# Forty products of the identity in TensorE's pauses of the first attention, and one early power on GpSimd

## The chip, the core and the metric

The kernel runs on one core of a Trainium2 chip. The core has five engines that run their own instruction streams and meet at semaphores: TensorE (PE in the profile; its weight loads are shown as PEld), VectorE (DVE), ScalarE (ACT), GpSimd (POOL) and SyncE (SP, which here only issues DMAs). The metric is the device time of one execution in microseconds; less is better. Times are given for the median of several executions, and the profile is of a single one.

## The reference

The first half is an attention between 512 tokens and 32 state rows for each of 8 batches and 8 heads of width 64, in both directions. Its output is rearranged to 4352 rows of 512 and goes through a gated feed-forward layer of width 1536.

```
scores = scale * x @ state^T            # B,H,512,32
xread  = softmax(scores) @ state
sread  = softmax(scale * state @ x^T) @ x
rows   = concat(xread, sread), heads joined        # (8*544, 512)
xn     = rows / sqrt(mean(rows^2) + 1e-6) * rms_g
out    = (silu(xn @ w_gate) * (xn @ w_val)) @ w_out
```

The weights come as 64-bit floating-point numbers and are turned into 32-bit ones on the chip.

## The kernel before

Batch 0 stands apart from the others, since the weights are still being fetched and converted while it runs. Its work is cut into streams, Python generators that issue a few instructions and yield. The string `ORDER` (lines 22 to 28) is the schedule, written out by hand: one letter is one step of one stream. TensorE, VectorE and ScalarE execute their instructions in exactly this order; each engine takes its own instructions one after the other, so one that waits holds up all behind it. GpSimd's and SyncE's instructions are placed by the framework.

The streams that matter here:

- `a`, `tokens_read(0)`: transposes the state rows (line 268) and the tokens (278), scores (287), a softmax over the 32 state rows (VectorE: 298 transposition, 307 maximum, 309, 318 sum, 320 to 323, 325 transposition back; ScalarE: 300 copy, 311 exponential), the read (332), and the mean square of the read: ScalarE squares (339), VectorE adds (342), TensorE sums over partitions (346), VectorE adds the epsilon (350), GpSimd raises to the power -1/2 (250), TensorE spreads the result along rows (257), and VectorE multiplies the weights of attention by it (356).
- `s`, `states_read(0)`: the softmax in the other direction (368 maximum, 374 exponential), its transposition (381) with the copy out (383), the read (393), its scaling (400), and a transposition (404, copied by 406).
- `e` and `d`, `exponents` and `values`: the conversion of 18 weight pieces, three steps on ScalarE (195, 197, 200) and four on VectorE (221, 224, 228, 233) for each piece. The raw pieces are loaded four ahead (166). ScalarE's and VectorE's halves of a piece meet in two buffers named `ex` and two named `top`; the first weights go to `w_m`, the output weights to `wo`, and converted `w_m` is also written to DRAM as `w_d` (237).
- `v`: the state rows times the converted weights (450), copied to `v` by ScalarE (461).
- `h`, `t`, `u`: gate and value products of one of the 12 blocks of the hidden layer from `aT_s` and `v` (492), silu (498), product of both (502).
- `p`: the projection to the output (690), accumulated in four PSUM banks taken from the pools `fx`, `fz`, `fx` and `fy` (687).
- `A` and `S`: the two attention streams of batch 1.

Batches 1 to 7 run in a second hand-written order, `PERIOD`, with a matrix product of seven block products instead of eight (lines 596 and 750), and the state rows of all batches follow at the end. PSUM banks named `at` and `pv` come two to a pool, so a product into a third one waits until the first has been copied out. The tile `ident` is the 128x128 identity for transpositions, built by GpSimd at the start; `mhalf` holds -1/2 and `ones` holds 1.

Of the kernel before, what the change touches and what calls it, by code (L numbers as in the profile page):

```python
# [8 lines left out]
F32 = mybir.dt.float32  # L9
# [3 lines left out]
ALU = mybir.AluOpType  # L13
# [4 lines left out]
P = 128  # L18
# [1 line left out]
W_BUFS = 3  # L20

ORDER = (
    "aaaaaaaaddaaaaaaeaseeaasadsassssdsaaaasaeadesaeeasdasaaeadeadaaaddeeasedaadsadae"
    "edvvavdadeaAhdeeddtdAdAAhueheAeedtddphAedvdvduvdphedeAedtdhApeehddeuAdddeAhdedvd"
    "tudvvpeAAAAdhdAAteAehuhpddephepdeAdAeApAdteedAAvvveAdpudAAephtdSdhAdphdeAueedhAd"
    "eAteudddeeSppAddAAdppAdAdevApvdveehhAdthAudhpdeddeedeAdteAupvdvdvphedAAtdShhutSA"
    "hpukSSSkkkwSwkpSkpwpSSckSScckkpcSwkkkwwww"
)

PERIOD = (  # L30
# [12 lines left out]
def kernel(  # L43
# [20 lines left out]
    VE, SE, GE, TE = nc.vector, nc.scalar, nc.gpsimd, nc.tensor  # L64
# [5 lines left out]
    NC = S // P  # L70
# [7 lines left out]
    consts = ctx.enter_context(tc.tile_pool(name="consts", bufs=1))  # L78
# [9 lines left out]
    fz = ctx.enter_context(tc.tile_pool(name="fz", bufs=1, space=PSUM))  # L88
# [11 lines left out]
    def load_state(b):  # L100

        rows[b] = two.tile([P, 2, D], F32, name="rows")
        for j in range(4):
            src = state[b, 2 * j:2 * j + 2].rearrange("e n d -> n e d")
            nc.sync.dma_start(out=rows[b][Ns * j:Ns * j + Ns], in_=src)
# [8 lines left out]
    ident = consts.tile([P, P], F32, name="ident")  # L114
    make_identity(nc, ident)
    mhalf = consts.tile([P, NC], F32, name="mhalf")
    GE.memset(mhalf, -0.5)
    ones = consts.tile([P, 1], F32, name="ones")
    GE.memset(ones, 1.0)
    bounds = consts.tile([P, 2], F32, name="bounds")  # L120
    GE.memset(bounds[:, 0:1], 1151.0 + 7.5 / 16)
    GE.memset(bounds[:, 1:2], 255.0 * (1 << 23))
# [58 lines left out]
    def exponents():  # L181

        for k in range(len(pieces)):
            for a in parts(k):
                if k not in raw:
                    yield from range(3)
                    continue
                if a.start == 0:  # L190
                    exs[k] = conv.tile([P, 8 * P], I32, name="ex")
                ex = exs[k][:, columns(k, a)]
                hi = raw[k][:, columns(k, a), 1]
                half = ex.bitcast(U16).rearrange("p (f two) -> p f two", two=2)[:, :, 1]
                SE.activation(out=ex.bitcast(F32), in_=hi.bitcast(F32), func=ACTF.Abs)
                yield
                SE.activation(out=ex, in_=half, func=ACTF.Relu, scale=-1.0 / 16,
                              bias=bounds[:, 0:1])
                yield
                SE.activation(out=ex, in_=ex, func=ACTF.Relu, scale=-float(1 << 23),  # L200
                              bias=bounds[:, 1:2])
                yield
# [235 lines left out]
    def own_weights(b, mp):  # L438


        pv = []

        def products():
            w = w_sb.pop(b * (NM // 2) + mp)
            for e in range(2):
                pv.append(vps.tile([P, 4 * P], F32, name="pv") if b and mp % 2 == 0 else
                          aps.tile([P, 4 * P], F32, name="at"))
            for j in range(4):
                for e in range(2):
                    TE.matmul(out=pv[e][Ns * j:Ns * j + Ns, :],  # L450
                              lhsT=stT_g[b][D * e:D * e + D, j, :],
                              rhs=w[D * e:D * e + D, j].rearrange("p m k f -> p (m k f)"),
                              start=True, stop=True)
            fetch(b * (NM // 2) + mp + W_BUFS)
            yield

        def copies():
            v = (seven["v"] if b else v_0).tile([P, 2, 2, 2, P], F32, name="v")
            v_sb[b, mp] = v, None
            for e in range(2):  # L460
                SE.copy(v[:, e].rearrange("p m k f -> p (m k f)"), pv[e])  # L461
                yield
            if b:
                more_of_v(b, mp)
                yield

        return products(), copies()
# [215 lines left out]
    def project_as_ready(banks):  # L683


        for f in (fx, fz, fx, fy):
            banks.append(f.tile([P, DM], F32, name="f"))

        def part(m, r):
            TE.matmul(out=banks[r], lhsT=hb[:, m, P * r:P * r + P], rhs=wo[:, m, :],  # L690
                      start=(m == 0), stop=(m == NM - 1))

        for m in range(NM - 2):
            for r in range(4):
                part(m, r)
                if r % 2:
                    yield
        for r in range(4):
            part(NM - 2, r)
            part(NM - 1, r)  # L700
            yield

    def projected(banks, store):
        spare = seven["s"].rearrange("p (r k) f -> p r (k f)", r=3)
        for r in range(4):
            ot = spare[:, r] if r < 3 else two.tile([P, DM], F32, name="ot", tag="g")
            SE.copy(ot, banks[r])
            store(r, 0, DM, ot)
            yield
# [11 lines left out]
    def weight_sums():  # L721

        t1, t2, t4 = (seven["t"][:, i] for i in range(3))
        for k in range(0, HM, 2):
            def blk(i, j):
                return wo[:, HM * i + k:HM * i + k + 2, HD * j:HD * j + HD]
            for dst, a, b in ((t1[:, k:k + 2], blk(0, 1), blk(0, 0)),
                              (t2[:, k:k + 2], blk(1, 1), t1[:, k:k + 2]),
                              (blk(0, 1), blk(1, 1), blk(0, 1)),
                              (t4[:, k:k + 2], blk(1, 0), t2[:, k:k + 2])):  # L730
                VE.tensor_tensor(out=dst, in0=a, in1=b, op=ALU.subtract)
                yield
# [81 lines left out]
    def store_tokens(b):  # L814
        def store(r, c0, n, ot):
            r0 = T * b + P * r
            nc.sync.dma_start(out=out[r0:r0 + P, c0:c0 + n], in_=ot)
        return store
# [7 lines left out]
    done = object()  # L826

    def of_batch_0(part):

        for m in range(NM):  # L830
            if m not in parts_0:
                parts_0[m] = hidden(m, lambda e, k, m=m: v_sb[0, m // 2][0][:, e, m % 2, k, :],
                                    [aT_s[0][:, e, :] for e in range(2)])
            yield from parts_0[m][part]

    def first_of_batch(b):
        for mp in range(2):
            for part in own_weights(b, mp):
                yield from part

    def first_products(b, own):
        slot_sums(b)
        yield
        for part in own:
            yield from part[0]
# [15 lines left out]
    for k in range(1, RAW_AHEAD):  # L861
# [3 lines left out]
    streams = {"a": tokens_read(0), "s": states_read(0), "A": tokens_read(1), "S": states_read(1),  # L865
               "e": exponents(), "d": values(),
               "v": (step for mp in range(NM // 2) for part in own_weights(0, mp) for step in part),
               "h": of_batch_0(0), "t": of_batch_0(1), "u": of_batch_0(2),
               "p": project_as_ready(banks_0), "c": projected(banks_0, store_tokens(0)),
               "w": first_of_batch(1), "k": weight_sums()}  # L870
    by_hand = dict(engines={mybir.EngineType.PE, mybir.EngineType.DVE,
                            mybir.EngineType.Activation})
    with tc.manual_schedule(**by_hand):
        for stream in ORDER:
# [2 lines left out]
                open_late()  # L877
                slot_sums(1)
            next(streams[stream])
    assert all(next(stream, done) is done for stream in streams.values())  # L880
    load_state(2)
    load_x(2)

    for b in range(1, B):
        if b + 2 < B:
# [3 lines left out]
        p, c, k = project_seven(S, store_tokens(b))  # L889
# [3 lines left out]
        streams = {"h": h, "t": t, "u": u, "p": p, "c": c, "k": k,  # L893
                   "v": (step for part in own for step in part[0]),
                   "x": (step for part in own + then for step in part[1])}
        if b + 1 < B:
            streams.update(a=tokens_read(b + 1), s=states_read(b + 1),
                           w=first_products(b + 1, then))
# [12 lines left out]
    p, c, k = project_seven(NT, store_states, nc.scalar)  # L911
    streams = {"h": h, "t": t, "u": u, "p": p, "c": c, "k": k, "y": sums_of_w(range(1, NM // 2))}
# [33 lines left out]
```

## Time and profile before

| | |
|---|---|
| median of six runs | 802.4 us |
| lowest, highest | 802.0, 803.26 us |
| profiled execution, device time | 803.26 us |
| its span, first to last instruction | 801.5 us |
| mean granted TensorE clock | 0.987 |
| TensorE busy | 776.5 us (97%) |
| VectorE busy | 515.0 us (64%) |
| ScalarE busy | 347.1 us (43%) |
| GpSimd busy | 178.0 us (22%) |

A slice of the page's picture is one fortieth of the span, 20 us. A digit is the busy share of an engine in tenths; the row PEclk is the granted TensorE clock in tenths of full speed. The profile counts the passes of a product: one 32-bit product makes two passes, so eight products of line 450 are written "x16". A row of the timeline gives start and length in us, engine, line, what is written from what, and in square brackets the engine's idle time ahead of it and what ended it. Ends of matrix products are modelled, so rows that follow one another overlap a little.

### The profile page before, as it was taken

The page shows a single profiled execution, that of the slowest core. Times are in us where ns is not written, and L with a number is a line of the kernel's source. Part 1 is how long each engine was busy: PE and PEld are TensorE (multiplying, and loading weights), DVE is VectorE, ACT ScalarE, POOL GpSimd, SP SyncE. Part 2 cuts the span into 40 slices and gives each one's busy share as a digit, 9 for nine tenths or more (in the row PEclk, how much of TensorE's full clock was granted, in tenths as well). Part 3 has the DMA queues.
Part 4 walks back from the last instruction along what each step waited for, and adds up shares of the span by engine and source line. Part 5 has one row for each costly group of instructions (what it writes and reads, how often), then busy time and mean ns, then how long its engine had stood idle before and what let it go on. Part 6 is the DMA issues. An engine that isn't in the chain of part 4 may idle for free.

```text
span 801.5 us, 12112 instructions
## 1 busy us (share of the span) xinstructions
PE 776.5 (97%) x4822; PEld 594.2 (74%) x4822; DVE 515.0 (64%) x786; ACT 347.1 (43%) x572; POOL 178.0 (22%) x215
## 2 busy tenths in 40 slices
PE   4599999999999999999999999999999999999998
PEld 2244444788878887888778887888788877888996
DVE  4989996588337851787358833785178735891461
ACT  5888874563145322542246314532254224510320
POOL 0000003530145004510443014500451044400000
PEclk9589999999999999999999999999999999999999
DMA  9788744710182006500361008200540025101311
GB/s 294 232 272 311 265 160 163 247 67 0 33 287 105 1 16 205 204 1 14 100 237 75 1 30 287 108 1 14 172 184 2 13 104 179 74 0 47 112 54 27
DMA packets 61592, 94.11 MB, mean 117 GB/s; under 512 B 38752, under 2 KB 46432, under 8 KB 54624
## 3 DMA queue, kind: packets, MB, share of 16 engines
q1 hardware_dynamic: 59360, 92.75, 33.7%
q8 instruction: 38, 0.62, 0.3%
q10 hardware_dynamic: 2176, 0.59, 0.3%
q14 instruction: 18, 0.15, 0.1%
HBM read 78.12 MB, written 15.20 MB: 116 GB/s over the span
## 4 chain that ended last, share of the span: by engine, by line
PE 94%; DVE 4%; issue 0%; ACT 0%; DMA 0%; SPq 0%; DVEq 0%
PE f L596 37%; PE f L750 35%; PE f L690 5%; PE pv L492 4%; PE at L450 3%; PE pv L450 3%; PE at L278 2%; PE at L287 1%; PE at L332 1%; PE at L346 1%; PE at L393 1%; DVE ex L228 1%; PE at L381 1%; DVE raw L224 1%; PE at L257 1%
## 5 line engine op out<-in xcount | busy, mean ns | idle before, releaser
L750 PE MATMUL f<-wo,hb 128*128 128x256 f32 x540 | 124.2, 382 | 0.4 <-ACT ot L787 0.2
L658 DVE TENSOR_TENSOR g<-g,f 128x512 f32<-128x512 f32 (+1 forms) x96 | 62.7, 654 | 90.1 <-PE f L596 86.6
L596 PE MATMUL f<-aT_s,v 128*128 128x256 f32 x504 | 119.5, 380 | 0.0
L750 PEld LDWEIGHTS f<-wo,hb 128*128 128x128 f32 x540 | 101.4, 190 | 20.1 <-ACT ot L787 6.9
L596 PEld LDWEIGHTS f<-aT_s,v 128*128 128x128 f32 x504 | 93.8, 190 | 17.4 <-issue 5.2
L250 POOL TENSOR_TENSOR ri<-ss,mhalf 128x4 f32<-128x4 f32 x8 | 9.1, 1142 | 365.5 <-DVE ss L350 365.5
L596 PE MATMUL f<-aT_t,vs 128*128 128x256 f32 x336 | 87.2, 382 | 0.0
L750 PE MATMUL f<-wt,hs 128*128 128x256 f32 x360 | 80.4, 379 | 0.0
L649 ACT ACTIVATE hb<-g 128x1024 f32<-128x1024 f32 (+1 forms) x48 | 48.2, 1004 | 63.0 <-DVE g L658 63.0
L750 PEld LDWEIGHTS f<-wt,hs 128*128 128x128 f32 x360 | 68.3, 190 | 9.5 <-issue 0.2
L787 ACT COPY ot<-f 128x256 f32<-128x256 f32 x60 | 21.5, 372 | 122.6 <-PE f L750 122.6
L596 PEld LDWEIGHTS f<-aT_t,vs 128*128 128x128 f32 x336 | 62.6, 190 | 15.1 <-issue 5.9
L661 DVE SCALAR_TENSOR_TENSOR hb<-hb,g 128x1024 f32<-128x1024 f32 x42 | 55.5, 1322 | 7.8 <-ACT hb L649 7.8
L647 ACT COPY g<-f 128x512 f32<-128x512 f32 (+1 forms) x48 | 26.9, 560 | 76.7 <-PE f L596 76.7
L479 POOL TENSOR_TENSOR vs<-v,vs 128x256 f32<-128x256 f32 x42 | 58.4, 1390 | 0.0
L476 POOL TENSOR_TENSOR vs<-v 128x256 f32<-128x256 f32 x42 | 30.6, 729 | 118.4 <-ACT v L461 118.4
L492 PE MATMUL pv<-aT_s,v 128*128 128x512 f32 x96 | 46.1, 621 | 1.1 <-DVE aT_s L356 1.1
L690 PE MATMUL f<-wo,hb 128*128 128x512 f32 x96 | 44.7, 600 | 0.0
L596 PE MATMUL f<-aT_t,v 128*128 128x256 f32 x168 | 43.9, 383 | 0.0
L596 PE MATMUL f<-aT_s,vs 128*128 128x256 f32 x168 | 43.1, 379 | 0.0
L750 PE MATMUL f<-wt,hb 128*128 128x256 f32 x180 | 42.6, 386 | 0.0
L750 PE MATMUL f<-wo,hs 128*128 128x256 f32 x180 | 41.6, 382 | 0.0
(128 smaller groups left out, 1237.9 us busy)
## 6 DMA issues: line engine op xcount, KB each, us to landing
w_m<-w_d SPq DMA_DIRECT2D x48, 1024.0 KB, 6.7
x_b<-in_x_dram SPq DMA_DIRECT2D x30, 256.0 KB, 4.1
out_dram<-ot SPq DMA_DIRECT2D x56, 128.0 KB, 1.8
raw<-in_moe_w_val_dram SPq DMA_DIRECT2D x6, 1024.0 KB, 5.2
raw<-in_moe_w_out_dram SPq DMA_DIRECT2D x6, 1024.0 KB, 7.2
w_d<-w_m SPq DMA_DIRECT2D x6, 1024.0 KB, 4.9
raw<-in_moe_w_gate_dram SPq DMA_DIRECT2D x5, 1024.0 KB, 5.7
raw<-in_moe_w_gate_dram SPq DMA_DIRECT2D x2, 512.0 KB, 4.8
```

Of the source, the lines that this page charges most:

```text
L450: TE.matmul(out=pv[e][Ns * j:Ns * j + Ns, :], lhsT=stT_g[b][D * e:D * e + D, j, :], rhs=w[D * e:D * e + D, j].rearrange("p m k f -> p (m k ...
L476: GE.tensor_tensor(out=vs[:, 0], in0=a21, in1=a22, op=ALU.add)
L479: GE.tensor_tensor(out=vs[:, 2], in0=a12, in1=vs[:, 1], op=ALU.subtract)
L492: TE.matmul(out=to[0], lhsT=lhs(i, k), rhs=r, start=(i == 0), stop=(i == len(rhs) - 1))
L596: TE.matmul(out=ps[:, i, 0:half], lhsT=l[:, i, :], rhs=r, start=(start and i == 0 and k == 0), stop=(k == len(lhs) - 1), skip_group_check= ...
L647: SE.copy(gates(q)[1], q["x"][:, :, 0:half])
L649: SE.activation(out=hb[:, 2 * mp:2 * mp + 2, 0:n].rearrange("p m (c t) -> p m c t", c=2), in_=q["g"][:, :, :, 0:half], func=ACTF.Silu if s ...
L658: VE.tensor_tensor(out=to, in0=to, in1=q[ps][:, :, 0:half], op=ALU.add)
L661: VE.scalar_tensor_tensor(out=h, in0=h, scalar=1.0, op0=ALU.add, op1=ALU.mult, in1=q["g"].rearrange("p m c t -> p m (c t)"))
L690: TE.matmul(out=banks[r], lhsT=hb[:, m, P * r:P * r + P], rhs=wo[:, m, :], start=(m == 0), stop=(m == NM - 1))
L750: TE.matmul(out=banks[name][:, r, :], lhsT=lhs(k)[:, P * r:P * r + P], rhs=rhs(k), start=(start and r == 0 and k == 0), stop=(k == HM - 1) ...
L787: SE.copy(to, banks[name][:, r, :])
```

## The change

`ORDER` gets 40 letters `z` in eight groups; without them it is the same string. A `z` step issues one product of the identity with itself, written twice side by side (128x256), into a PSUM tile of the pool `fz`. Nothing reads that tile. The pool's tile is taken by the projection later, after the last `z`. On TensorE's own stream the forty stand as follows: 14 after line 287, 2 after 381, 7 after 393, 4 after 332, 5 after 404, 2 after 346, 2 after 450, and 4 after 268 (the transposition of batch 1's state rows, which follows line 257). All other instructions of TensorE, VectorE and ScalarE keep their order.

GpSimd gets one more instruction, a power of a constant (1 to the -1/2, 128x4), after the identity is built and ahead of the first power of line 250. Nothing reads its result. On SyncE's queue, one of the two later loads of tokens for batch 2 (`x_b`) comes to stand before the first write of `w_d` instead of after three more weight pieces.

Line numbers in the text are those of the kernel before.

```
 ORDER = (
-    "aaaaaaaaddaaaaaaeaseeaasadsassssdsaaaasaeadesaeeasdasaaeadeadaaaddeeasedaadsadae"
-    "edvvavdadeaAhdeeddtdAdAAhueheAeedtddphAedvdvduvdphedeAedtdhApeehddeuAdddeAhdedvd"
...
+    "aaaaaaaaddaaaaaaeaseeaasadsasszzzzzzzzzzzzzzssdsaaaasaeadesaeeazzsdasaaezzzzzzza"
+    "deadaaaddeeazzzzsedaadszzzzzadaeedzzvvavdzzadeaAzzzzhdeeddtdAdAAhueheAeedtddphAe"
...
 )
@@
     ones = consts.tile([P, 1], F32, name="ones")
     GE.memset(ones, 1.0)
+
+    GE.tensor_tensor(out=consts.tile([P, NC], F32, name="first_pow"), in1=mhalf,
+                     in0=ones.to_broadcast([P, NC]), op=ALU.pow)
@@
+    def keep_awake():
+
+
+        ps = fz.tile([P, 2, P], F32, name="f")
+        while True:
+            TE.matmul(out=ps, lhsT=ident, rhs=ident.unsqueeze(1).to_broadcast([P, 2, P]),
+                      start=True, stop=True)
+            yield
+
@@
-               "w": first_of_batch(1), "k": weight_sums()}
+               "w": first_of_batch(1), "k": weight_sums(), "z": keep_awake()}
@@
-    assert all(next(stream, done) is done for stream in streams.values())
+    assert all(next(stream, done) is done for name, stream in streams.items() if name != "z")
```

More of the change, by code (lines that the diff above doesn't have):

```diff
@@ L22 @@
 ORDER = (
-    "aaaaaaaaddaaaaaaeaseeaasadsassssdsaaaasaeadesaeeasdasaaeadeadaaaddeeasedaadsadae"
-    "edvvavdadeaAhdeeddtdAdAAhueheAeedtddphAedvdvduvdphedeAedtdhApeehddeuAdddeAhdedvd"
-    "tudvvpeAAAAdhdAAteAehuhpddephepdeAdAeApAdteedAAvvveAdpudAAephtdSdhAdphdeAueedhAd"
-    "eAteudddeeSppAddAAdppAdAdevApvdveehhAdthAudhpdeddeedeAdteAupvdvdvphedAAtdShhutSA"
-    "hpukSSSkkkwSwkpSkpwpSSckSScckkpcSwkkkwwww"
+    "aaaaaaaaddaaaaaaeaseeaasadsasszzzzzzzzzzzzzzssdsaaaasaeadesaeeazzsdasaaezzzzzzza"
+    "deadaaaddeeazzzzsedaadszzzzzadaeedzzvvavdzzadeaAzzzzhdeeddtdAdAAhueheAeedtddphAe"
+    "dvdvduvdphedeAedtdhApeehddeuAdddeAhdedvdtudvvpeAAAAdhdAAteAehuhpddephepdeAdAeApA"
+    "dteedAAvvveAdpudAAephtdSdhAdphdeAueedhAdeAteudddeeSppAddAAdppAdAdevApvdveehhAdth"
+    "AudhpdeddeedeAdteAupvdvdvphedAAtdShhutSAhpukSSSkkkwSwkpSkpwpSSckSScckkpcSwkkkwww"
+    "w"
 )
```

## The prediction

> **What bounds it.** I read the page's slices and its chain of waits first, then the granted clock and busy time in 5 us stretches, then TensorE's and VectorE's instructions in order of time up to 64 us.
>
> ```profile
> PE   4599999999999999999999999999999999999998
> ...
> DVE  4989996588337851787358833785178735891461
> ...
> PEclk9589999999999999999999999999999999999999
> ...
> PE 94%; DVE 4%; issue 0%; ACT 0%; DMA 0%; SPq 0%; DVEq 0%
> ```
>
> TensorE is full from the third slice (40 us) to the end, and the chain that ends last lies 94% on it. So a microsecond won before TensorE becomes the bound is won at the end, and nothing can be won later. The chain in order of time shows where that begins:
>
> ```profile
> 62.37 1.24 DVE w_m L233
> 63.61 0.14 issue
> 63.74 1.09 PE at L450 x16
> ```
>
> Before 63.74 the chain goes mostly through VectorE (it converts the weights, lines 221 to 233), after it through TensorE without a break. The question is how much earlier the third L450 can start. VectorE is busy over 4.8 of each 5 us from 15 to 35, and has one large gap:
>
> ```profile
> 35.00:40.00 5.00, 3.09 (x15) 1.76 (x8) 4.52 (x5) 4.46 (x6) 0.41 (x1) 0.50 0.97 333
> 40.00:45.00 5.00, 5.00 (x11) 2.38 (x10) 3.58 (x5) 3.41 (x5) 0.00 (x0) 0.58 0.51 167
> 45.00:50.00 5.00, 5.00 (x16) 2.39 (x15) 4.35 (x5) 4.34 (x6) 0.00 (x0) 1.00 0.96 296
> ...
> 28.06 0.69 DVE L342 TENSOR_TENSOR sq<-sq 128x512 f32<-128x512 f32 x1
> ...
> 37.34 1.22 DVE L356 TENSOR_TENSOR aT_s<-aT_s,at 128x1024 f32<-128x1024 f32 x1 [0.41 <-PE at L257]
> ...
> 45.61 0.69 DVE L502 TENSOR_TENSOR hb<-t,pv 128x512 f32<-128x512 f32 x1 [2.00 <-PE pv L492]
> ```
>
> The columns of a stretch are busy PE, weight loads, DVE, ACT, POOL, then clock and DMA. VectorE waits for TensorE twice, 0.41 and 2.00 us, and TensorE is then at half clock. The durations say that it was at half clock from the start, though the clock column reads 1.00 before about 23.7 except where an event changed it: the same transposition, early and late,
>
> ```profile
> L278 PE MATMUL at<-ident,x_b x16: 421/421/477, 5.3 to 8.8; 128*128 128x128 f32 x16
> ...
> L278 PE MATMUL at<-ident,x_b x12: 272/273/273, 47.1 to 61.5; 128*128 128x128 f32 x12
> ```
>
> (minimum, median, maximum ns, first and last start). L381 at 17.46 still takes 421. TensorE's pauses, in which the new products go:
>
> ```profile
> 9.87 1.96 PE L287 MATMUL at<-xT,stT 64*32 64x512 f32 x16 [0.68 <-ACT xT L280]
> 17.46 1.97 PE L381 MATMUL at<-ident,e 128*128 128x128 f32 x8 [5.63 <-ACT e L374]
> ...
> 31.36 1.84 PE L346 MATMUL at<-ones,sq 128*128 128x1 f32 x8 [2.31 <-DVE sq L342]
> 33.13 2.28 PE L450 MATMUL at<-w_m,stT_g 64*32 64x512 f32 x16
> 36.21 1.09 PE L257 MATMUL at<-ident,ri 128*128 128x128 f32 x4 [0.81 <-ACT v L461]
> ...
> 38.62 3.78 PE L492 MATMUL pv<-aT_s,v 128*128 128x512 f32 x4 [1.10 <-DVE aT_s L356]
> ```
>
> **The price of a product.** One fp32 product is two passes in the profile (two L492 products are "x4"). The chain has eight 512-column passes of L690 in 3.43 us: 0.43 us a pass. At 256 columns the twelve L596 passes at 146.02 start 0.215 us apart. So an added product takes 0.43 us at full clock and about 0.86 at half; its weight load (190 ns a pass, same shape in L596) hides below the pass. The 40 cost 17.2 us of TensorE at full clock, all ahead of the first L492 (38.62). [...] They wait for nothing; what they can delay is the real product behind them.
>
> **Group of 14.** L287 streams until about 11.6 (its last 0.2 us is latency: a pass of L492 lasts 592 ns at a spacing of 430). When does the clock rise? The trace's 3.41 us stretches between clock changes lie at 10.06, 13.47, 16.89, 20.30, 23.71 (fall) and 40.78, 44.20 (rise). In 16.89 to 20.30 TensorE was busy 2.84 us, in 40.78 to 44.20 all 3.42: full clock followed both. After 20.30 to 23.71 with 1.65 busy it fell; 37.37 to 40.78 with 2.31 did not raise it. With L287 and products 10.06 to 13.47 is filled, so I take full clock from 13.47: 2.2 products before it, 11.8 x 0.43 = 5.1 after, end 18.55, against L381's 17.46. L381 then takes 0.6 us to its first tile (3 x 0.107 + 0.273), ready at 19.15; ACT's L383, at 18.62 before, starts 0.6 late, and all of ACT behind it too. L311 (the second exponential) then ends at 20.3; VectorE takes it at 21.51. The conversion steps L195 to L200 end at 26.3; VectorE needs them at 28.67. Only L339 is near: it starts at 26.3 after L332, which at full clock ends at 24.83 + 1.04 = 25.9 (1.04 from the later run of L332 at 98.37). Its first pair ends at 27.4, and VectorE is free for L342 at 27.87 (L224 at 26.71 plus the 1.14 between such starts). Nothing is lost as long as ACT is no more than 1.1 us late.
>
> **Groups of 2 and 7.** L393's second half waits for L383 (20.8) and ends at 21.4; seven products end at 24.4, L332 can start at 24.83 as before. **Groups of 4 and 5:** 25.7 to 27.4, L404 at 28.0 (ACT frees its bank), products to 30.2; L346 comes after VectorE's last L342, 31.17. All inside pauses. **Then:** L346 0.8 us (its later run, 114.56) instead of 1.84, two products, L450 starts at 32.85 and ends near 34.2 (before 35.41), ACT's L461 frees the bank at 35.2, L257 done 35.9 (before 37.31), L268 and four products end at 37.5. VectorE is free for L356 at 36.65, 0.69 earlier than before (0.19 at L342, 0.5 at L356); L492 follows at 37.93, behind the last product.
>
> **The gate.** At full clock the first two gate products, the transposition and the value products take 1.72 + 0.43 + 1.72 = 3.9 us: L502 could start at 42.0. VectorE's conversions reach it at 42.93 + 0.62 - 0.69 = 42.86. So the 2.00 us wait goes, and VectorE is 0.69 + 2.06 = 2.75 us early. What is late next is VectorE itself: I carried TensorE on, and it comes to the third L450 at about 59.7, where the weights (L233) are ready at 60.9. ACT's L195 is tied to VectorE by its two buffers (L195 at 49.88 waits for L233) and moves with it. **Sum: 803.26 (the profiled execution: span 801.5 and 1.76 around it) - 2.75 = 800.5.** This execution is the slowest of the six; the median is 802.4. That fits the clock: a rise at 44.20 instead of 41.5 costs half of 2.7 us, about the spread 802.0 to 803.26. The changed kernel should lose this spread at the gate, but its first rise can fall later than 13.47, each us by 0.5 us at L381; I add 0.1: **800.6**.
>
> **Against the skill.** The Trainium skill, "TensorE: Matmul & The Clock Gate", Part 4, says that transposes don't count as busy for the clock. The row of 16.89 to 20.30 speaks against a strict reading: eight transpositions filled 1.9 of its 2.84 us and the clock rose. By the rule, though, only what follows L287 is sure: rise as late as 15 to 18.4, L381 at 19.3 to 21.0, ACT 1.4 to 3.1 late, the excess over 1.1 lost: 800.8 to 802.5. I side with the row, since the products are no transposes. The same page's Part 1 has the clock fall after an idle window of about 3.4 us. The row again is stricter: 1.65 of 3.41 busy was lost. By the rule the pauses left in the new order (0.9 us at most, ahead of L346) cost nothing; by the row 75% busy there lies between kept and lost; lost, L346 to L257 are cold again, L356 stays at 37.34, and the gain is 2.05.
>
> **First power.** POOL's first L250 takes 1.86 us, the others 1.02. The added one runs at about 1.4 us, where POOL is idle until 33.5, and takes 0.84 off the first L250. Worth: L257 waits for ACT (0.81) and VectorE's L233 covers it until 36.65; without the power L257 would end about 35.95. I count 0, at most 0.3 if that cover is thin. **SyncE:** one x_b load of batch 2 moves ahead of a w_d write and a weight load. 256 KB at some 400 GB/s is 0.65 us, at 27 to 33 us where the DMA engines have idle stretches; that weight piece is used ten us later. Cost 0.
>
> **Rivals.** (1) *Late or interrupted warm-up*, as above: 801.3 to 802.4, about 801.8. For it: the clock's windows may lie elsewhere in each execution. Chance 0.15. (2) *VectorE hides it*: conversions or their loads set the pace, only the 0.69 stays: 802.6. For it: VectorE over 4.8 of 5; against: its 2.00 us wait names L492. Chance 0.08. (3) *TensorE's whole lead counts*: 63.32 (its real arrival before) - 59.7 = 3.6: 799.7. Against: L450 needs L233. Chance 0.06. (4) *The change doesn't do what it says*: products of a mostly zero identity don't raise the clock. Then all 40 run at 0.86, 34.3 us in pauses of some 14; L381 moves to 23.6, L492 to about 57: 821. It turns to loss earlier: beyond 3.5 cold products in the first group each costs 0.43, so 10 of 14 cold eat the gain. Against: L287 is followed at once, and ordinary dense products did raise it at 44.20. Chance 0.12, reaching from 803 up.
>
> **Numbers.** Forecast 0.59, own range 800.1 to 801.1. 0.2% is 1.6 us, about what can be told from no change. Faster (below 800.8): 0.85 x 0.59, rival 3, a little of rival 1: 0.59. Same 0.29, slower 0.12 (rival 4). Range 799.7 to 802.3.
>
> **Signs.** Right: full-clock durations (273 ns for L381, 600 for L332 and L450), L381 near 18.6, L356 near 36.7, L502 near 42.9 without a wait, the third L450 near 61 and behind L233. Wrong: 421 ns at L381; VectorE waiting at L342; L492 behind its four products; a new wait between 43 and 61.

## The result, and the profile after

The changed kernel takes 800.82 us (median of 20 runs, 799.95 to 801.45) against 802.35 us (40 runs, 801.73 to 803.78): a ratio of 0.9978, 95% interval 0.9972 to 0.9983. It is 1.5 us faster, and 0.2 us above the forecast of 800.6. Its profiled execution took 800.21 us (span 798.4) where that of before took 803.26 (span 801.5).

Lines of the attention code are 4 higher in the profiles of the changed kernel (L346 is 342 before, L385 381, L454 450, L506 502), and 1 to 6 higher in the experiments; the added product is L845. The page's pictures first:

```profile
PE   6999999999999999999999999999999999999998
...
DVE  4999996688347842786358833785278635881461
...
PEclk9999999999999999999999999999999999999999
...
PE 92%; DVE 5%; DMA 1%; issue 0%; ACT 0%; SPq 0%
```

TensorE is full from the second slice on and its clock stands at full. The end is still set by TensorE. VectorE's waits at L356 and L502 (0.41 and 2.00 us before) are gone from its rows in order of time:

```profile
11.78 1.31 DVE L302 STREAM_TRANSPOSE eS<-at 128x512 f32<-128x512 f32 x2 [1.01 <-PE at L291]
...
27.74 0.67 DVE L346 TENSOR_TENSOR sq<-sq 128x512 f32<-128x512 f32 x1
...
36.38 1.21 DVE L360 TENSOR_TENSOR aT_s<-aT_s,at 128x1024 f32<-128x1024 f32 x1
...
42.56 0.68 DVE L506 TENSOR_TENSOR hb<-t,pv 128x512 f32<-128x512 f32 x1
```

And TensorE's, with the products of the identity among the real ones:

```profile
5.97 0.45 PE L272 MATMUL at<-ident,rows 128*128 128x128 f32 x1 [5.97 <-DMA rows<-in_state_dram]
6.22 3.70 PE L282 MATMUL at<-ident,x_b 128*128 128x128 f32 x16
10.59 1.09 PE L291 MATMUL at<-xT,stT 64*32 64x512 f32 x16 [0.68 <-ACT xT L284]
11.62 6.31 PE L845 MATMUL f<-ident 128*128 128x256 f32 x28
17.77 1.04 PE L385 MATMUL at<-ident,e 128*128 128x128 f32 x8
...
37.65 1.98 PE L496 MATMUL pv<-aT_s,v 128*128 128x512 f32 x4 [0.17 <-DVE aT_s L360]
...
60.66 1.09 PE L454 MATMUL at<-w_m,stT_g 64*32 64x512 f32 x16 [0.89 <-DVE w_m L237]
```

The third L454 starts at 60.66 instead of 63.74, 3.08 us earlier, and the span is 3.1 us shorter: what was won there is won at the end. Two rows were not foreseen. The first transposition waits for the state rows until 5.97, where it was 5.08. And L291 already runs at full clock (1.09 us, before 1.96): the first change of the clock that this trace records is its rise at 10.15 us, ahead of the first added product. The two nearly cancel at L302, 11.78 against 11.91.

### The profile page after: what moved, and what is told of

Read it like the earlier page. It is cut to its first block, busy times and chain, and to the rows that moved or that the text cites. A ratio compares the mean times of both kernels' runs of the same rounds, so it can differ in the third digit from the quotient of the medians.

```text
span 798.4 us, 12273 instructions
## 1 busy us (share of the span) xinstructions
PE 785.2 (98%) x4902; PEld 604.6 (76%) x4902; DVE 514.7 (64%) x786; ACT 347.0 (43%) x572; POOL 179.1 (22%) x216
## 4 chain that ended last, share of the span: by engine, by line
PE 92%; DVE 5%; DMA 1%; issue 0%; ACT 0%; SPq 0%
PE f L600 37%; PE f L754 35%; PE f L694 5%; PE pv L496 3%; PE at L454 3%; PE pv L454 3%; PE at L282 2%; PE at L291 1%; DVE ex L232 1%; PE at L397 1%; PE at L336 1%; DVE raw L228 1%; PE at L385 1%; PE at L350 1%; DMA raw<-in_moe_w_gate_dram 1%; DVE w_m L237 1%
## 5 line engine op out<-in xcount | busy, mean ns | idle before, releaser
L496 PE MATMUL pv<-aT_s,v 128*128 128x512 f32 x96 | 43.7, 594 | 0.2 <-DVE aT_s L360 0.2
```

The lines of the kernel that those rows point to most:

```text
L496: TE.matmul(out=to[0], lhsT=lhs(i, k), rhs=r, start=(i == 0), stop=(i == len(rhs) - 1))
```

## The experiments

All are compared with the kernel before on the same chip; ratios are to it. Runs of one set share their runs of before.

### The early power and the products, each by itself

```
power_alone:     ORDER without the letters z
products_alone:
-    GE.tensor_tensor(out=consts.tile([P, NC], F32, name="first_pow"), in1=mhalf,
-                     in0=ones.to_broadcast([P, NC]), op=ALU.pow)
```

> Only the early power, no products of the identity. Theory (the whole gain is the clock at the gate): no change, 802.2 to 802.5 us, the first power of line 250 takes 1.02 instead of 1.86 us and VectorE's L356 still starts near 37.3, since L257 waits for ScalarE. Rival (the power carries part of it): up to 0.8 us faster, 801.6.

> All 40 products, no early power. Theory: as the changed kernel, 800.7 to 801.0 us; the first power takes 1.86 us, and VectorE's L237 (233 in the kernel before) covers it until about 36.4. Rival (the power is on the path once the clock is up): 801.3 to 801.7.

The power alone took 803.09 us, ratio 1.001 (1.0001 to 1.0019): slightly slower. The products alone took 800.48, ratio 0.9974 (0.9965 to 0.9983): the whole gain is theirs. Both theories of the power were wrong. GpSimd's rows in order of time for `power_alone`, and for the changed kernel the durations of its powers (minimum, median, maximum ns):

```profile
1.38 1.03 POOL L121 TENSOR_TENSOR first_pow<-ones,mhalf 128x4 f32<-128x4 f32 x1
...
33.31 1.93 POOL L253 TENSOR_TENSOR ri<-ss,mhalf 128x4 f32<-128x4 f32 x1 [30.91 <-DVE ss L353]
```

```profile
L254 POOL TENSOR_TENSOR ri<-ss,mhalf x8: 1018/1019/1982, 33.0 to 644.5; 128x4 f32<-128x4 f32 x8
```

The first power on the core takes 1.03 us, as the later ones do; the power at 33 us still takes 1.9. So the 1.86 us of before was no cost of a first use, and the early power has nothing to take away. What goes with the long one: VectorE has started a 1024-column instruction with two inputs (line 224, 1.2 us) 0.1 to 0.2 us ahead of it; at the second power, near 114 to 117 us, beside other VectorE work, it is 1.16 us. That the two engines slow each other there was not tried by itself.

What comes with the power shows at the start: the first transposition starts at 5.95 with it and at 5.17 in `products_alone`.

### What delays the state rows

The power's result is a 16-byte tile in the pool `consts`, and the layout of the built program puts it ahead of nearly all others: the state rows move from byte 90880 of a partition to 90912, the tokens from 91904 to 91936. One run keeps the power and gives its tile 64 bytes; one replaces the power by a fill of the small tile.

```
power_aligned:
-    out=consts.tile([P, NC], F32, name="first_pow")
+    out=consts.tile([P, 16], F32, name="first_pow")[:, 0:NC]
shift_alone:
-    GE.tensor_tensor(out=consts.tile([P, NC], F32, name="first_pow"), in1=mhalf, ...)
+    GE.memset(consts.tile([P, NC], F32, name="first_pow"), 0.0)
```

> The changed kernel, with the power's result tile 64 bytes a partition instead of 16, so that all tiles behind it lie 64 bytes later than in the kernel before, not 32. If the place of the load targets is what delays the state rows and tokens at the start: the first transposition (L272) starts near 5.1 us instead of 5.97, x_b loads land in 4.1 to 4.2 us instead of 4.7, and the time is as without the power, 800.3 to 800.6. If it is the power instruction itself: L272 near 5.95, x_b 4.7, 800.8 to 801.0.

> The changed kernel, with a fill of the 16-byte tile in place of the power: tiles lie 32 bytes later, no power early. If the place is the cause: first transposition near 5.95 us, x_b loads 4.7 us, 800.8 to 801.0. If the power instruction is the cause: 5.1 us, 4.2 us, 800.3 to 800.6.

They took 800.97 us (0.9978, 0.9969 to 0.9987) and 801.15 us (0.998, 0.9971 to 0.9988). TensorE's first row in each, the fill ahead of the 64-byte tile:

```profile
5.98 0.45 PE L271 MATMUL at<-ident,rows 128*128 128x128 f32 x1 [5.98 <-DMA rows<-in_state_dram]
```

```profile
6.09 0.45 PE L272 MATMUL at<-ident,rows 128*128 128x128 f32 x1 [6.09 <-DMA rows<-in_state_dram]
```

Without a power the rows are as late as with it, so the power instruction is not needed for the delay; and 64 bytes are no better than 32, so my guess of 64 as the measure was wrong. The load table over the first 12 us, before and after (count, size, median us to landing), shows it in the loads of short rows:

```profile
x_b<-in_x_dram SPq DMA_DIRECT2D x3, 256.0 KB, 4.1
x_b<-in_x_dram ACTq DMA_DIRECT2D x2, 256.0 KB, 3.2
rows<-in_state_dram SPq DMA_DIRECT2D x8, 16.0 KB, 6.4
```

```profile
x_b<-in_x_dram SPq DMA_DIRECT2D x3, 256.0 KB, 5.0
x_b<-in_x_dram ACTq DMA_DIRECT2D x2, 256.0 KB, 3.8
rows<-in_state_dram SPq DMA_DIRECT2D x8, 16.0 KB, 7.1
```

The weights, in long rows, land within 0.1 us of the same times in both, and the state rows' loads are issued from 0.74 us on in both, so it is the transfer that takes longer. Tokens and states are moved in rows of 64 floats, 256 bytes. Before, the targets started at a multiple of 256 (90880 = 355 x 256); in the profiles of all ten kernels with a tile added the first transposition starts at 5.87 to 6.11 us, in three without one (before, `products_alone`, `head_4`) at 5.08 to 5.21. The Trainium skill's "DMA: Bandwidth & Descriptors", "How a descriptor splits into AXI transactions", has an access begin at a 256-byte boundary, so that a row across one costs an access more. The page says it of reads, and the shifted side here is the written one, so that it holds there is an inference. It fits both shifts; a shift by a whole 256 bytes was not tried, so the place is the likely cause, not a shown one.

### Which products count

```
first_14:    only the first group of z is kept in ORDER
without_14:  only the first group is left out
```

> Only the first group of 14 products stays. Theory: full clock for L381 to L332, then the clock falls in the pauses from 21 to 36 us and the gate products run at half clock as before; at most the 0.2 to 0.3 us at L342 are kept: 802.0 to 802.4 us. Rival (an early rise is enough, the clock holds through the pauses): 800.8.

> The first group of 14 is left out, the other 26 stay. Theory: L381 and the first products run at half clock, the clock rises near 20 to 24 us and stays; the gate is as in the changed kernel, with 0 to 0.5 us lost at L342: 800.8 to 801.4 us. Rival (the first group is what counts): 802.2 or more.

The first 14 alone: 803.95 us, 1.0015 (1.0006 to 1.0024), slower. The other 26 alone: 800.94 us, 0.9984 (0.9975 to 0.9992), most of the gain. In the profile of the first 14, the first transpositions of the second direction are at full clock and the gate is not:

```profile
17.69 1.04 PE L384 MATMUL at<-ident,e 128*128 128x128 f32 x8
...
38.42 3.78 PE L495 MATMUL pv<-aT_s,v 128*128 128x512 f32 x4 [1.10 <-DVE aT_s L359]
```

L384 takes 1.04 us, and L495 its 3.78 us at half clock, as before the change; VectorE waits 1.86 us for it. The clock fell at 23.25 in this execution. In the profile of the other 26 L384 starts at 18.33 and takes 1.97 us, and L495 takes 1.98 us at 38.65. So full clock behind the first group alone is worth little, and a clock that holds until the gate is nearly all. The 803.95 is 1.6 us above the upper end of what I expected; some 0.7 of it is the added tile, as in `power_alone`. In its profile the rest lies behind the last copy: the third product of line 450 starts at 63.39 (before 63.74), the last copy ends at 797.91, and the span at 802.7, 4.8 us later; in the changed kernel this tail is 3.2 us. The 1.6 us are in the issue of the last two stores on ScalarE's queue, 2.45 us there against 0.85 in the changed kernel and before. Why it takes longer stays open.

### What the clock counts

```
transposes:
-            TE.matmul(out=ps, lhsT=ident, rhs=ident.unsqueeze(1).to_broadcast([P, 2, P]), ...)
+            for k in range(4):
+                TE.transpose(out=ps[:, k % 2, :], in_=ident, identity=ident)
zeros:       rhs=zero.unsqueeze(1).to_broadcast([P, 2, P])     (zero: a tile of 0.0)
narrow:      TE.matmul(out=ps[:, 0, :], lhsT=ident, rhs=ident, start=True, stop=True)
```

> Each product is replaced by four transpositions of the identity (0.43 us at full clock, as one product). If transpositions count as activity for the clock, as the stretch from 16.89 to 20.30 of the kernel before suggests: 800.6 to 801.1 us. If they do not, as the skill's page says: the first group runs at half clock throughout, L381 comes near 23 us, and the time is over 805.

> The products multiply the identity by a tile of zeros, same shape and number. If the clock follows the instructions: 800.6 to 801.1 us, L385 (381 before) in 273 ns a pass. If it follows the data that move through the array (the fourth rival's reason): half clock, over 805.

> The same 40 products with 128 columns instead of 256, so half the fill (8.6 us). Theory (a stretch of 3.4 us must be mostly busy): the clock is lost in some of the pauses and regained late, 801.2 to 802.2 us. Rival (little activity holds it): 800.8.

Transpositions: 801.05 us, 0.9978 (0.9969 to 0.9987). Zeros: 801.05 us, 0.9977 (0.9968 to 0.9987). Both are the changed kernel's gain, so transpositions count as activity, and so do products of zeros. Half as wide: 801.52 us, 0.9984 (0.9975 to 0.9994), with the widest spread, 800.13 to 802.58. Its profile has the clock lost and found again; a stretch's columns are length, busy PE, weight loads, DVE, ACT, POOL, then clock, DMA share and GB/s:

```profile
28.30:31.71 3.41, 1.45 (x11) 1.26 (x11) 3.38 (x6) 3.34 (x5) 0.00 (x0) 1.00 0.91 323
31.71:35.12 3.41, 3.24 (x20) 2.86 (x28) 3.33 (x7) 2.73 (x3) 1.12 (x1) 0.50 0.46 181
35.12:38.54 3.42, 3.42 (x25) 1.94 (x10) 2.29 (x2) 1.89 (x4) 0.80 (x1) 0.50 0.96 286
24.88:28.30 3.42, 2.20 (x22) 1.20 (x22) 3.35 (x5) 2.63 (x5) 0.00 (x0) 1.00 0.40 80
```

A stretch with 1.45 us busy of 3.41 lost the clock, one with 2.20 kept it. The second row is the odd one: 3.24 us busy, and the clock did not rise after it; it holds L350, eight passes of one column. The cost is on VectorE: L360 waits 1.27 us for L261 and starts at 38.71 instead of 36.38; 0.86 of these 2.33 us are there at L302 already, since the clock's first rise fell late in this execution, at 14.64.

### How full the pauses are

```
fourteen_to_22:  eight more z in the first group
```

> Eight more products in the first group: 3.44 us more on TensorE ahead of L385 (381 before). Theory (pauses were filled to the brim, ScalarE may be 1.1 us later than before at most): ScalarE 3.2 us later, VectorE loses about 2.1 us at its second sum and at L346: 802.9 us (802.3 to 803.3), slower than before or equal. Rival (slack to spare): 800.8.

It took 803.31 us, 1.0008 (0.9997 to 1.002), the loss of the whole gain, within 0.4 us of the 802.9 expected. Five executions lie at 802.20 to 802.58 and five at 804.05 to 804.85; the profile is of one of the faster five (802.47, first rise at 9.71). VectorE's rows in order of time show the two places that were named:

```profile
22.94 0.69 DVE L322 TENSOR_REDUCE z<-eS 128x16 f32<-128x512 f32 x1 [1.55 <-ACT eS L315]
...
29.94 0.69 DVE L346 TENSOR_TENSOR sq<-sq 128x512 f32<-128x512 f32 x1 [0.52 <-ACT sq L343]
```

1.55 + 0.52 = 2.07 us of new waits on ScalarE, which sits behind L385; L346 starts at 29.94 instead of 27.74. So in this execution 3.44 us of products cost 2.2 us: the slack behind L385 was 1.2 us (I had 1.1). The slower five have no trace.

### Four or eight products at the start

Both leave the power and its tile out.

```
head_4:   ORDER = "zzzz" + ORDER
head_8:   ORDER = "zzzzzzzz" + ORDER
```

> All 40 products without the power, and four more at the very start, while TensorE waits for the first state rows. At half clock they take 0.86 each from about 1.5 us, so they end at about 5.0, as the rows land (5.1). If the first rise of the clock still falls late in some executions of the changed kernel, these four move it ahead of L291 (287 before) in all of them: 799.6 to 800.0 us, and a narrower spread than without them. If the early loads or VectorE's first conversion (raw piece at 9.6 us) set the pace, no change: 800.4.

> As the kernel with four at the start, with eight. They end between 6.7 and 8.4 us and push the first transposition back by 1.6 to 3.3 us, though all that follows then runs at full clock. Theory: some of the delay reaches VectorE, 800.2 to 801.2, slower than with four. Rival (token loads and copies are the bound until 9 us): 799.6.

Four at the start: 799.72 us (5 runs, 799.4 to 800.42), 0.9965 (0.9953 to 0.9978), the best of all. Its interval meets that of the changed kernel only at its end, and overlaps that of `products_alone`, so that the four gain anything over the products alone is not shown. Eight: 800.79 us, 0.9976 (0.9966 to 0.9986): the first transposition starts at 7.72 and L299 (298 before) at 12.22, against 10.75 with four; so the rival, that the loads are the bound until 9 us, fell. In the profile with four, at 800.42 the slowest of its runs, the clock rose at 4.82 but was lost once more:

```profile
29.99 1.02 PE L347 MATMUL at<-ones,sq 128*128 128x1 f32 x8 [0.98 <-DVE sq L343]
...
31.91 1.84 PE L451 MATMUL at<-w_m,stT_g 64*32 64x512 f32 x16
```

```profile
28.71:32.12 3.41, 2.43 (x22) 1.75 (x28) 3.37 (x7) 2.73 (x3) 0.11 (x1) 1.00 0.80 239
...
32.12:35.54 3.42, 3.42 (x20) 1.40 (x5) 3.28 (x3) 2.96 (x5) 1.81 (x1) 0.50 0.98 310
```

The stretch from 28.71 held the 0.98 us pause ahead of L347 and L347's own eight one-column passes, and 2.43 us busy did not keep the clock. VectorE then waited 0.75 us at L357. This is the interrupted warm-up of the prediction, priced at 0.7.

## Why the prediction was right

**The bound and the exchange at the third L450.** Right. It starts behind L233's weights, at 60.66 where about 60.9 was worked out, and the gain there is the gain in the span. TensorE has waited 0.89 us for them, so it came at 59.77, where 59.7 was worked out.

**The price of a product.** Right: 28 passes lasted 6.31 us with the last one's latency, 0.22 each; all 40 ran at full clock in the profiled execution, and all lay in pauses.

**The sum.** The steps against the measured times of VectorE, earlier than before: L342 0.19 worked out, 0.32 measured; L356 0.69 and 0.96; L502 2.75 and 3.05. The gate was the large term, 2.06 worked out and 2.09 measured; of the 0.3 us that the sum was short, 0.13 are there at L302 already. `first_14` and `without_14` show that the large term hangs on the clock at the gate, and `products_alone` that the power has no part in it. The moved load of tokens was not tried by itself: it moves with the products in `products_alone` and `without_14`, and stays in `power_alone` and `first_14`. In the traces before and after no engine waits for a load between 11 us and the third L450, which speaks against a part of it. (The later run of L332 that gave 1.04 us starts at 98.30, not 98.37.)

**The clock's rise.** I took 13.47 us, by products after L287, with L287 at half clock. In the profiled execution the sixteen transpositions ahead of it were enough, and L385 starts at 17.77 where 18.55 was worked out. The changes of the clock in each trace lie on a grid of 3.41 us; carried back, it puts these stretches around the transpositions, before and after:

```profile
6.65:10.06 3.41, 2.73 (x20) 2.06 (x26) 0.42 (x1) 2.10 (x4) 0.00 (x0) 1.00 0.94 314
```

```profile
6.74:10.15 3.41, 3.18 (x15) 2.37 (x13) 0.51 (x3) 1.95 (x4) 0.00 (x0) 1.00 1.08 316
```

Behind 3.18 us the clock rose, behind 2.73 it did not (the 1.00 in these rows is the column's reading ahead of the first recorded change). In `zeros`, `transposes` and `shift_alone` no stretch ahead of the added products held more than 2.75 us of work; the rise fell at 14 to 15.4 us, L291 took 1.96 us, and their spans are 799.3 to 800.0 instead of 798.4. So both happen, by where the grid falls in an execution, and the 1.5 us of spread that I meant to have removed at the gate is still there. In the traces it lies at L291; with late rows and a late rise VectorE comes to the gate's L506 at 43.46 us (`transposes`), with an early rise at 42.56. The executions of the changed kernel show the same two cases in their times: nine lie at 799.95 to 800.43, ten at 800.95 to 801.45, one between. The median of 800.82 falls into the gap, so that it is only 0.2 us from the forecast is in part luck.

**The first power.** This part was wrong twice, though I counted it 0. It was to take 0.84 us off the first L250; that still takes 1.98 us. And it was to cost nothing; with its tile the first transposition starts 0.8 to 0.9 us later, and `power_alone` is 0.74 us slower than before. Where both rise early, the tile costs 0.6 us at L302 (11.78, and 11.18 in `products_alone`) and 0.5 us of the span (798.4, and 797.9). On the sum this was offset in the profiled execution by L291 at full clock. Over the runs it is the term that was missing: the products alone are at 800.48, just below the forecast, the whole change at 800.82, just above.

**Why 803.26 stood above the median.** I put it down to a late rise at the gate. The runs of before show another part: in the set run beside `head_4`, those with a mean granted clock of 0.987 took 803.27 to 803.75 us, those with 0.981 or 0.983 took 801.67 to 802.8. 0.987 is the clock of the profiled execution, whose trace first shows full clock at 20.3 us, after L287; `power_alone`, at 0.983, has a first rise at 10.3 us and L290 (287 before) at 1.09 us. Between the two profiled executions this part is nearly gone, since the late rise before and the late rows after cancel at L302. The profile of `power_alone` is the closer comparison: the same tile, an early rise, L301 (298 before) at 11.75, and no products.

```profile
45.65 0.69 DVE L505 TENSOR_TENSOR hb<-t,pv 128x512 f32<-128x512 f32 x1 [2.19 <-PE pv L495]
```

Its L505 starts 3.09 us after the 42.56 of the changed kernel, and its span is 3.1 us longer. So in this pair the products are worth 3.1 us, a little more than the 2.75 worked out; in the medians they are worth 2.3 us with the tile (803.09 to 800.82) and 1.9 us without it (802.35 to 800.48), and the whole change 1.5 us. The executions nearest the medians of before have no trace, so where they lose less than the profiled one stays open. To subtract the gain from the slowest of six executions and to compare with a median was the weak step; the reason given for it, a spread that the change removes, did not hold.

**What the rules on the clock would have made.** `transposes` shows that transpositions do hold the clock here; by the strict reading of Part 4 of the Trainium skill's "TensorE: Matmul & The Clock Gate" the forecast would have been 800.8 to 802.5. The clock fell after stretches with 1.45, 1.65 and 2.43 us busy; the idle window of that page's Part 1 was too mild.

**The rivals.** Late or interrupted warm-up is seen in single executions (`narrow`, `head_4`), at about the price given. The fourth, that the identity's zeros don't raise the clock, fell with `zeros`. The second, that VectorE hides the gain, fell too: VectorE does set the third L450, but at 60.66 instead of 63.74. The third counted TensorE's whole lead; the 0.89 us wait for the weights ended that.

## What to carry to other kernels

Filler products paid here at one place, where TensorE at half clock made another engine wait on the chain that ends last; the rest of the fill only had to hold the clock until there, and a product too many costs its full time once the pause is full. A tile added for a trick moves all tiles behind it, and can cost more than the trick brings: compare where the loads land and when the first one does. A first instruction that takes long has not been shown to pay for a first use until an earlier use has been put ahead of it.

## What was not expected of the hardware

- Transpositions alone raise the clock: 3.18 us of them in 3.41 us did at 10.15 us, 2.73 us before did not, and the kernel with transpositions in place of products is as fast (801.05 us).
- A stretch with 2.43 us of TensorE work lost the clock (`head_4`) and one with 2.20 us kept it; one with 3.24 us did not raise it (`narrow`) and one with 2.80 did (`without_14`, at 21.13 us). The odd ones held the eight one-column passes, 1.02 us of the 2.43 and all but 1.4 of the 3.24. Without these passes the stretches of all fourteen traces up to 52 us sort: the clock fell after at most 1.69 us (`first_14`) and held from 1.74 on (`without_14`); at half clock it rose after at least 2.80 and stayed low up to 2.75. That one-column passes count for next to nothing is read from this sorting; it was not tried by itself.
- Loads of 256-byte rows land later once their targets lie 32 or 64 bytes off a multiple of 256: tokens 5.0 us instead of 4.1 over the first 12 us. That the place is the cause is likely, not shown.
- The same small power takes 1.03 us early, 1.02 us late, and 1.86 to 2.0 us at 32 to 34 us, with or without a power before it.
